# The second MLP product of five token groups by Strassen's identity, with its sums on VectorE and GpSimd

## The chip, the cores and the metric

The kernel runs on one core of a Trainium2 chip. The metric is the device time of one execution in microseconds (us). The profile's own time is its span, from the first to the last instruction of one profiled execution. The engines are TensorE (PE, whose weight loads are listed as PEld), VectorE (DVE), ScalarE (ACT), GpSimd (POOL) and SyncE (SP), which only issues transfers here.

## The reference

A block-wise linear attention with decay feeds a two-layer MLP. Batch 4, 8 heads, 768 positions, head size 64; the MLP sees 3072 tokens of width 512 and has 2048 hidden units.

```
for b in range(nb):                              # per head, blocks of positions
    intra = (q_b @ k_b.T * Dmask) @ v_b          # Dmask[i, j] = lam ** (i - j) for i >= j
    out_b = intra + (q_b * lam ** (pos + 1)) @ state
    state = lam ** block * state + (k_b * lam ** (block - 1 - pos)).T @ v_b
x = out as 3072 x 512                            # heads side by side
g = gelu(x @ w_in)                               # w_in 512 x 2048, exact gelu
result = g @ w_out                               # w_out 2048 x 512, f32
```

## The kernel before

The tokens are cut into 24 chunks of 128, six to a batch element, and four chunks make a group (`M = 4`, `NG = 6` groups of 512 tokens). A group's attention output, transposed, is `xT[g]`, four tiles of 128 features by 512 tokens in bf16.

`mlp_blocks(g)` gives the MLP of a group as a list of blocks, each with a cost by which the work is ordered. The first product has 16 blocks, `mm1(kf)`: four matmuls of 128x512 into a PSUM bank (L288) and a Gelu on ScalarE into `g_t`, bf16, 16 tiles of 128 hidden units by 512 tokens (L290). The second product takes `g_t` as the weights of PE and `w_out_t` as the moving operand: for each chunk of 128 tokens, 16 matmuls of 128x512 (L300), a copy to SBUF on ScalarE (L305) and a store of 256 KB on SP's queue (L306). The last chunk of the last group is done in two halves of 256 columns (L315, L319, L320).

Attention for group g + 1 is woven into the MLP of group g. The order of all instructions is that in which the code writes them; nothing is rescheduled, so each engine runs its own part of that one order as its queue, and waits on semaphores. The main loop runs through the blocks, adds up their costs in `done`, and emits a step of attention when `done` passes its mark. Marks are fractions of a group's total cost. For chunk n, the i-th of its group, with `at = 0.06 + 0.245 * i`:

- kind 0, at `at - 0.32` (earlier in the group before for small i): `dma_transposes` has SP transpose k (L189), GpSimd scale q to `q_hat` (L190), and SP transpose that (L191); GpSimd decays k to `k_dec` (L167); `prefetch` issues the three loads of a chunk three further on from GpSimd (L65).
- kind 2, at `at`: `scores` (PE L198; the masks on VectorE, L202) and `next_state` (PE L238; VectorE L245 and L246).
- kind 3, one chunk later (0.965 for the last): `outputs` (PE L253, L263), emptied by a cast on VectorE into `xT[g + 1]` (L273).

PSUM has eight banks: two each for the tags `sc`, `mh` (first product) and `mo` (second product), one for `o` (attention output) and one for `t` (state). Group 0 has another order, written out by hand, and its own weaving of the attention of group 1; it isn't touched.

Of the kernel before, what the change touches and what calls it, by code (L numbers as in the profile page):

```python
# [8 lines left out]
F32 = mybir.dt.float32  # L9
BF16 = mybir.dt.bfloat16  # L10
ALU = mybir.AluOpType
# [4 lines left out]
def kernel(  # L16
# [10 lines left out]
    nc = tc.nc  # L27

    B, H, S, D = q.shape
    d_model, d_ff = moe_w_in.shape  # L30
# [18 lines left out]
    work_pool = ctx.enter_context(tc.tile_pool(name="work", bufs=3))  # L49
    x_pool = ctx.enter_context(tc.tile_pool(name="x", bufs=2))  # L50
    g_pool = ctx.enter_context(tc.tile_pool(name="g", bufs=2))
    out_pool = ctx.enter_context(tc.tile_pool(name="outp", bufs=3))
    ps = ctx.enter_context(tc.tile_pool(name="ps", bufs=1, space=bass.MemoryType.PSUM))


# [92 lines left out]
    def bank(shape, dtype, tag, name):  # L148
        return ps.tile(shape, dtype, tag=tag, name=name, bufs=2 if tag in ("sc", "mh", "mo") else 1)
# [123 lines left out]
            nc.vector.tensor_copy(c.x_o, c.o_ps)  # L273


    def mlp_blocks(g):
        T = M * C
        x_t = xT[g]
# [16 lines left out]
        def mm2(io, part):  # L295
            def run():
                if part == 0:
                    om[io] = bank([128, d_model], F32, "mo", "o2_ps")
                for kf in range(part * 4, part * 4 + 4):
                    nc.tensor.matmul(om[io], g_t[:, kf, io * C:(io + 1) * C], w_out_t[:, kf, :],  # L300
                                     start=(kf == 0), stop=(kf == NK2 - 1))
                if part == NK2 // 4 - 1:
                    o_sb = out_pool.tile([128, d_model], F32, tag="o_s", name="o_sb")
                    r = (g * M + io) * C
                    nc.scalar.copy(o_sb, om[io])  # L305
                    nc.sync.dma_start(out[r:r + C, :], o_sb)  # L306
            return run

        def mm2_half(io, half):

            def run():
                w = slice(half * (d_model // 2), (half + 1) * (d_model // 2))
                o2 = bank([128, d_model // 2], F32, "mo", "o2_ps")
                for kf in range(NK2):
                    nc.tensor.matmul(o2, g_t[:, kf, io * C:(io + 1) * C], w_out_t[:, kf, w],  # L315
                                     start=(kf == 0), stop=(kf == NK2 - 1))
                o_sb = out_pool.tile([128, d_model // 2], F32, tag="o_h", name="o_sb")
                r = (g * M + io) * C
                nc.scalar.copy(o_sb, o2)  # L319
                nc.sync.dma_start(out[r:r + C, w], o_sb)  # L320
            return run

        parts = NK2 // 4
        blocks = [(mm1(kf), 4 * T) for kf in range(NK2)]
        if g == 0:

            blocks += [(mm2(io, part), 4 * 512) for pair in range(0, M, 2) for part in range(parts)
                       for io in (pair, pair + 1)]
        else:
            last = g == NG - 1  # L330
            blocks += [(mm2(io, part), 4 * 512) for io in range(M - last) for part in range(parts)]
            if last:
                blocks += [(mm2_half(M - 1, half), 16 * 256) for half in range(2)]
        return blocks


# [84 lines left out]


    total = NK2 * 4 * M * C + M * NK2 * 512
    x1 = lambda n: outputs(live[n], xT[1], n - M)
    group0 = {
        1: [lambda: next_state(live[3])],
# [12 lines left out]
    for n in range(2 * M, NCH):  # L439
        g, i = n // M - 1, n % M  # L440
        at = 0.06 + 0.245 * i
        fs = [at - (0.18 if n == 2 * M else 0.32), None, at, at + 0.245 if i < M - 1 else 0.965]
        todo += [(round((g + f) * total), -kind, n) for kind, f in enumerate(fs) if f is not None]
    todo.sort()

    def step(minus_kind, n):
# [58 lines left out]
```

## Time and profile before

| | |
|---|---|
| three runs | 217.22, 218.49, 219.40 us; median 218.49 |
| span of the profiled execution | 217.5 us; no time of that execution other than its span is given |
| PE busy | 204.9 us, 94% |
| PE weight loads busy | 102.9 us, 47% |
| GpSimd busy | 105.8 us, 49% |
| ScalarE busy | 91.1 us, 42% |
| VectorE busy | 74.8 us, 34% |
| mean granted TensorE clock | 0.997 |
| groups 1, 2, 3, 4, 5 start at | 54.0, 89.2, 121.6, 153.8, 186.2 us |

Busy times are unions of the instructions' intervals on an engine. A matmul's own duration in the trace (0.377 us for 128x512) is longer than its share of the time, since matmuls overlap in the array; the price of a matmul in a stream is the distance of two starts. "Idle before" a group of instructions is followed by what ended the idle time. GpSimd's work is front-loaded: it runs ahead as far as its buffers let it, and has nothing left to do after 152 us.

### The profile page before, as it was taken

The page shows a single profiled execution, that of the slowest core. Times are in us where ns is not written, and L with a number is a line of the kernel's source. Part 1 is how long each engine was busy: PE and PEld are TensorE (multiplying, and loading weights), DVE is VectorE, ACT ScalarE, POOL GpSimd, SP SyncE. Part 2 cuts the span into 40 slices and gives each one's busy share as a digit, 9 for nine tenths or more (in the row PEclk, how much of TensorE's full clock was granted, in tenths as well). Part 3 has the DMA queues.
Part 4 walks back from the last instruction along what each step waited for, and adds up shares of the span by engine and source line. Part 5 has one row for each costly group of instructions (what it writes and reads, how often), then busy time and mean ns, then how long its engine had stood idle before and what let it go on. Part 6 is the DMA issues. An engine that isn't in the chain of part 4 may idle for free.

```text
span 217.5 us, 3545 instructions
## 1 busy us (share of the span) xinstructions
PE 204.9 (94%) x1422; PEld 102.9 (47%) x1446; DVE 74.8 (34%) x120; ACT 91.1 (42%) x169; POOL 105.8 (49%) x120
## 2 busy tenths in 40 slices
PE   7679999999987999999999999999999999999993
PEld 2355444555443544444545444544445545444452
DVE  5884000478516243316225323315415323100000
ACT  6975772434563321365221375221465221566121
POOL 8998333998999999276950809113000000000000
PEclk9999999999999999999999999999999999999998
DMA  5999999999999999999999497515251012100112
GB/s 37 149 169 203 198 194 183 156 208 148 177 150 126 164 128 138 215 110 104 109 114 160 77 180 62 37 48 146 74 98 24 3 57 88 50 0 3 48 49 96
DMA packets 100272, 24.35 MB, mean 112 GB/s; under 512 B 92960, under 2 KB 97312, under 8 KB 100256
## 3 DMA queue, kind: packets, MB, share of 16 engines
q0 software_dynamic: 79104, 13.64, 84.4%
q1 hardware_dynamic: 21152, 10.50, 22.7%
q8 instruction: 11, 0.18, 0.3%
q14 instruction: 5, 0.04, 0.1%
HBM read 27.27 MB, written 6.29 MB: 154 GB/s over the span
## 4 chain that ended last, share of the span: by engine, by line
PE 73%; DMA 14%; POOL 9%; issue 2%; ACT 0%; POOLq 0%
PE o_ps L300 33%; PE h_ps L288 28%; DMA q_t<-in_q_dram 8%; DMA qT<-q_hat 3%; DMA w_in_t<-in_moe_w_in_dram 3%; PE o_ps L263 3%; PE sc_ps L198 3%; POOL k_t L65 3%; POOL q_t L65 2%; POOL v_t L65 2%; PE kv_ps L238 2%; PE o_ps L315 2%; PE o_ps L253 2%; POOL k_dec L167 1%; POOL q_hat L190 1%
## 5 line engine op out<-in xcount | busy, mean ns | idle before, releaser
L288 PE MATMUL h_ps<-x_t,w_in_t 128*128 128x512 bf16 (+2 forms) x378 | 84.8, 377 | 1.0 <-DMA w_in_t<-in_moe_w_in_dram 0.5
L300 PE MATMUL o_ps<-w_out_t,g_t 128*128 128x512 bf16 x355 | 81.8, 379 | 0.8 <-issue 0.3
L290 ACT ACTIVATE g_t<-h_ps 128x512 bf16<-128x512 f32 x96 | 57.3, 597 | 35.3 <-PE h_ps L288 35.3
L288 PEld LDWEIGHTS <-w_in_t 128*128 128x128 bf16 x388 | 37.3, 98 | 43.8 <-DMA w_in_t<-in_moe_w_in_dram 0.6
L300 PEld LDWEIGHTS <-g_t 128*128 128x128 bf16 x368 | 34.7, 98 | 39.6
L305 ACT COPY o_sb<-o_ps 128x512 f32<-128x512 f32 x23 | 13.5, 586 | 68.3 <-PE o_ps L300 62.5
L202 DVE TENSOR_TENSOR sc_m<-sc_ps,dmask 128x512 bf16<-128x512 f32 x48 | 30.8, 683 | 16.1 <-PE sc_ps L198 15.8
L273 DVE CAST x_t<-o_ps 128x512 bf16<-128x512 f32 x16 | 11.1, 692 | 71.4 <-PE o_ps L263 71.4
L190 POOL TENSOR_TENSOR q_hat<-q_t,lam_p 128x512 bf16<-128x512 bf16 x16 | 16.9, 1056 | 20.0 <-DMA qT<-q_hat 19.0
L167 POOL TENSOR_TENSOR k_dec<-k_t,lam_m 128x512 bf16<-128x512 bf16 x16 | 17.7, 1106 | 14.0 <-PE kv_ps L238 8.1
L65 POOL DMA_DIRECT2D k_t<-in_k_dram x24 | 22.1, 920 | 4.0 <-DMA w_out_t<-in_moe_w_out_dram 2.1
L65 POOL DMA_DIRECT2D q_t<-in_q_dram x24 | 21.5, 897 | 4.2 <-DMA w_out_t<-in_moe_w_out_dram 3.4
L65 POOL DMA_DIRECT2D v_t<-in_v_dram x24 | 21.4, 894 | 3.4 <-DMA w_out_t<-in_moe_w_out_dram 1.7
L198 PE MATMUL sc_ps<-qT,kT 64*128 64x128 bf16 x192 | 9.5, 218 | 3.8 <-DMA qT<-q_hat 2.6
L246 DVE TENSOR_TENSOR state<-tmp,lam_blk 128x512 bf16<-128x512 f32 x13 | 12.1, 932 | 0.5
L183 DVE TENSOR_TENSOR qT<-t_ps,lam_q 128x512 bf16<-128x512 bf16 x8 | 5.5, 689 | 18.9 <-PE t_ps L174 18.7
L263 PE MATMUL o_ps<-sc_m,v_t 128*64 128x128 bf16 x192 | 10.1, 225 | 0.0
L198 PEld LDWEIGHTS <-kT 64*128 64x128 bf16 x192 | 5.7, 94 | 8.3 <-issue 4.7
L361 PE MATMUL idle_ps<-idle 128*128 128x512 bf16 x21 | 7.5, 473 | 1.2 <-DVE idle L94 1.2
L245 DVE TENSOR_TENSOR tmp<-kv_ps,state 128x512 f32<-128x512 f32 x12 | 8.2, 681 | 0.0
L180 ACT COPY kT<-t_ps 128x512 bf16<-128x512 bf16 x7 | 4.1, 579 | 9.4 <-PE t_ps L174 9.4
L263 PEld LDWEIGHTS <-v_t 128*64 128x64 bf16 x192 | 6.2, 109 | 3.3 <-issue 0.8
(57 smaller groups left out, 82.7 us busy)
## 6 DMA issues: line engine op xcount, KB each, us to landing
out_dram<-o_sb SPq DMA_DIRECT2D x23, 256.0 KB, 2.6
k_t<-in_k_dram POOLq DMA_DIRECT2D x24, 128.0 KB, 4.6
q_t<-in_q_dram POOLq DMA_DIRECT2D x24, 128.0 KB, 5.9
v_t<-in_v_dram POOLq DMA_DIRECT2D x24, 128.0 KB, 5.9
w_in_t<-in_moe_w_in_dram POOLq DMA_DIRECT2D x4, 512.0 KB, 7.9
w_out_t<-in_moe_w_out_dram POOLq DMA_DIRECT2D x4, 512.0 KB, 15.1
kT<-k_t SPq DMA_TRANSPOSE x16, 4.7
qT<-q_hat SPq DMA_TRANSPOSE x16, 4.0
```

The lines of the kernel that those rows point to most:

```text
L65: nc.gpsimd.dma_start(raw[n, name], chunk_of(name, n))
L167: eng.tensor_mul(c.k_dec, c.k, scale[:, :, None].to_broadcast((128, H, D)))
L190: nc.gpsimd.tensor_mul(q_hat, c.q, lam_p[:, :, None].to_broadcast((128, H, D)))
L198: nc.tensor.matmul(sc_ps[hi][:, hp, :], c.kT[p, hp, :], c.qT[p, hp, :], start=True, stop=True)
L202: nc.vector.tensor_mul(c.sc_m[:, :, hi, :], sc_ps[hi], dmask_r[:, :, hi, :])
L246: nc.vector.tensor_mul(new, tmp, lam_blk)
L263: nc.tensor.matmul(o_ps[hi * D:(hi + 1) * D, hp, :], c.v[:, 2 * hp + hi, :], c.sc_m[:, hp, hi, :], start=(c.sb == 0 and hp == 0), stop=Tru ...
L273: nc.vector.tensor_copy(c.x_o, c.o_ps)
L288: nc.tensor.matmul(h_ps[:, lo:hi], w_in_t[:, ki, kf * 128:(kf + 1) * 128], x_t[:, ki, lo:hi], start=(ki == 0 and lo == 0), stop=(ki == NK1 ...
L290: nc.scalar.activation(g_t[:, kf, :], h_ps, ACT.Gelu)
L300: nc.tensor.matmul(om[io], g_t[:, kf, io * C:(io + 1) * C], w_out_t[:, kf, :], start=(kf == 0), stop=(kf == NK2 - 1))
L305: nc.scalar.copy(o_sb, om[io])
```

## The change

The second product of groups 1 to 5 is a product of a 512 x 2048 and a 2048 x 512 matrix. The changed kernel cuts each into four blocks: tokens into halves of 256 (`lo`, `hi`), hidden units into halves of 1024 (8 tiles of 128, `KH = 8`), output columns into halves of 256 (`DH`). Instead of eight block products it forms seven, each 16 matmuls of 128x256: two token tiles `u`, eight k tiles. The factors are sums of blocks. Sums of `w_out` blocks (five, numbered 1, 3, 4, 6, 7) are formed once, on VectorE, in group 1, in two pieces each of 128 x 1024 elements. Sums of `g_t` blocks (five, numbered 1, 2, 5, 6, 7) are formed in every group on VectorE, in four pieces of 128 x 512 elements each, emitted behind the blocks of the first product whose Gelus they need; the last four pieces come behind the first half of product 3. All are bf16.

The products run in the order 3, 4, 5, 2, 1, 6, 7. In PSUM, 3 and 5 accumulate in one bank (`p`), 4 and 2 in one (`q`), 1 and 7 in one (`r`), and 6 has its own (`s`); `p` and `q` are banks of the tag `mo`, `r` and `s` of `mh`, which the next group's first product uses too. ScalarE copies a bank out when a product ends, and the same bank goes on with the next product while the copied value is used in f32 sums: four additions or subtractions of 128 x 512 elements a group, on VectorE in group 1 and on GpSimd in groups 2 to 5. The last two additions of a group read PSUM and are done on VectorE. A group stores two halves of 256 tokens (512 KB each) when product 6 and product 7 are done; in the last group the first half is stored in two parts. The marks of attention steps are fractions of the new, smaller total cost of a group (`place`).

```diff
-    out_pool = ctx.enter_context(tc.tile_pool(name="outp", bufs=3))
+    out_pool = ctx.enter_context(tc.tile_pool(name="outp", bufs=2))
+    sum_pool = ctx.enter_context(tc.tile_pool(name="sums", bufs=1))
...
+    W_SUMS = {1: (B11, B22, ALU.add), 3: (B12, B22, ALU.subtract), 4: (B21, B11, ALU.subtract),
+              6: (B11, B12, ALU.add), 7: (B21, B22, ALU.add)}
+    def w_out_sum(i, half):
...
+        nc.vector.tensor_tensor(wsum[i][:, half * n:(half + 1) * n, :], w_out_t[:, at(ka), da], w_out_t[:, at(kb), db],
+                                op=op)
...
+        G_SUMS = {6: (0, hi, 0, lo, ALU.subtract), 1: (0, lo, KH, hi, ALU.add), 2: (0, hi, KH, hi, ALU.add),
+                  5: (0, lo, KH, lo, ALU.add), 7: (KH, lo, KH, hi, ALU.subtract)}
+        def g_sum(i, k):
...
+            nc.vector.tensor_tensor(gsum[i][:, k:k + 2, :], g_t[:, ka + k:ka + k + 2, ta], g_t[:, kb + k:kb + k + 2, tb],
+                                    op=op)
+        def with_sums(kf, run):
+            def both():
+                run()
+                done = kf - 2
+                if done >= 1 and done % 2 == 1:
+                    if done < KH:
+                        g_sum(6, done - 1)
+                    else:
+                        for i in (5, 1, 2, 7):
+                            g_sum(i, done - 1 - KH)
+                if g == 1 and 2 <= kf < 12:
+                    w_out_sum(*w_sums_left.pop(0))
+            return both
...
+        def late_sums():
+            for i in (5, 1, 2, 7):
+                g_sum(i, KH - 2)
...
+        def product(i, u, key, begin):
+            o = banks[key][:, u, :]
+            for k in range(KH):
+                nc.tensor.matmul(o, left[i](k, slice(u * C, (u + 1) * C)), right[i](k),
+                                 start=(begin and u == 0 and k == 0), stop=(k == KH - 1), skip_group_check=True)
+        adder = nc.vector if g == 1 else nc.gpsimd
...
+        def m3(u):
...
+            product(3, u, "p", True)
+            if u == 0:
+                late_sums()
+            else:
+                nc.scalar.copy(tile_f("e"), banks["p"])
+        def m4(u):
...
+            product(4, u, "q", True)
+            if u == 1:
+                nc.scalar.copy(tile_f("f"), banks["q"])
+                adder.tensor_add(sb["e"], sb["e"], sb["f"])
+        def m5(u):
+            product(5, u, "p", False)
+            if u == 1:
+                sb["o0"] = out_pool.tile([128, 2, d_model], F32, tag="o0", name="o0_sb")
+                nc.scalar.copy(sb["o0"][:, :, d_hi], banks["p"])
+                adder.tensor_sub(sb["f"], sb["e"], sb["o0"][:, :, d_hi])
+                if last:
+                    store(0, sb["o0"], d_hi)
+        def m2(u):
+            product(2, u, "q", False)
+            if u == 1:
...
+                nc.scalar.copy(sb["o1"][:, :, d_lo], banks["q"])
+                adder.tensor_sub(sb["e"], sb["e"], sb["o1"][:, :, d_lo])
+        def m1(u):
...
+            product(1, u, "r", True)
+            if u == 1:
+                nc.scalar.copy(tile_f("m"), banks["r"])
+                adder.tensor_add(sb["m"], sb["m"], sb["e"])
+        def m6(u):
+            product(6, u, "s", True)
+            if u == 1:
+                nc.vector.tensor_add(sb["o1"][:, :, d_hi], banks["s"], sb["m"])
+                store(1, sb["o1"])
+        def m7(u):
+            product(7, u, "r", False)
+            if u == 1:
+                nc.vector.tensor_add(sb["o0"][:, :, d_lo], banks["r"], sb["f"])
+                store(0, sb["o0"], d_lo if last else slice(0, d_model))
+        blocks += [((lambda f=f, u=u: f(u)), KH * DH) for f in (m3, m4, m5, m2, m1, m6, m7) for u in range(2)]
...
-            last = g == NG - 1
-            blocks += [(mm2(io, part), 4 * 512) for io in range(M - last) for part in range(parts)]
-            if last:
-                blocks += [(mm2_half(M - 1, half), 16 * 256) for half in range(2)]
+        if g > 0:
+            return blocks_by_seven(g, g_t, blocks)
...
+    later = NK2 * 4 * M * C + 7 * 2 * KH * DH
+    def place(at):
+        g, f = int(at), at - int(at)
+        return round(f * total) if g == 0 else round(total + (g - 1 + f) * later)
...
-        todo += [(round((g + f) * total), -kind, n) for kind, f in enumerate(fs) if f is not None]
+        todo += [(place(g + f), -kind, n) for kind, f in enumerate(fs) if f is not None]
```

## The prediction

> **What bounds the kernel now.** I read the view by stages first, cut at the starts of the groups (columns: window, its length, then busy us and instruction count of each engine, granted TensorE clock, DMA share, GB/s).
>
> ```profile
> core 0: us, PE busy (x) PEld busy (x) DVE busy (x) ACT busy (x) POOL busy (x), PEclk, DMA share, GB/s
> 54.00:89.20 35.20, 32.43 (x219) 16.03 (x221) 14.01 (x19) 11.90 (x20) 32.61 (x35) 1.00 2.00 148
> 89.20:121.60 32.40, 32.19 (x218) 15.82 (x221) 12.60 (x19) 11.90 (x20) 19.52 (x21) 1.00 1.21 129
> 121.60:153.80 32.20, 31.99 (x214) 15.62 (x217) 10.82 (x17) 11.90 (x20) 12.83 (x14) 1.00 0.68 90
> 153.80:186.20 32.40, 32.08 (x218) 15.90 (x221) 11.50 (x18) 11.90 (x20) 0.00 (x0) 1.00 0.22 58
> 186.20:214.10 27.90, 27.72 (x143) 13.96 (x143) 0.00 (x0) 12.32 (x22) 0.00 (x0) 1.00 0.12 43
> ```
>
> From group 2 on PE is never idle for more than 0.4 us a group, so every microsecond of matmul removed there is a microsecond of span, as long as nobody else becomes late. Group 1 (54.0 to 89.2) is different: GpSimd is busy for 32.6 of its 35.2 us, and PE lost 2.8 us there (2.2 of it a wait for a transposing DMA). Next, the chain that ended last (start, length, what) and the page's row of the wide products, for the price of a matmul:
>
> ```profile
> 186.35 3.02 PE h_ps L288 x14
> 189.43 10.74 PE h_ps L288 x49
> 200.22 10.31 PE o_ps L300 x47
> 210.53 3.51 PE o_ps L315 x32
> 214.06 0.37 ACT o_sb L319
> ```
>
> 10.31/47 = 0.219 us is a little high because a record is missing; 48 matmuls of 512 columns in 10.31 us make 0.215. The 32 matmuls of 256 columns take 3.51/32 = 0.110 us each, each with its own weight load, so halving the width halves the price.
>
> **What the change takes from PE.** Per group the second product goes from 64 x 0.215 = 13.8 us to 112 x 0.110 = 12.3 us: 1.5 us in groups 1 to 4, 1.55 in group 5, together **-7.6 us**. I trust this term to 0.5 us.
>
> **What it adds to VectorE, and where that is late.** Per group 20 sums of 512 bf16 elements (five sums in four pieces) and two additions from PSUM; in group 1 also ten weight sums of 1024 elements and four f32 additions. No row shows an addition of two bf16 tiles. The bounds:
>
> ```profile
> L167 DVE TENSOR_TENSOR k_dec<-k_t,lam_k 128x512 bf16<-128x512 bf16 x1 | 0.7, 681 | 0.0
> L138 DVE TENSOR_TENSOR dmask<-cmask,lam_m 128x1024 f32<-128x1024 f32 x1 | 1.2, 1225 | 0.8 <-ACT lam_m L124 0.8
> L182 DVE COPY kT<-t_ps 128x512 bf16<-128x512 bf16 x1 | 0.4, 416 | 0.0
> ```
>
> L167 has an f32 factor and costs 0.68 for 512 elements; L182, whose operands are all bf16 as in the new sums, costs 0.42. I take L182's pace, and for 1024 elements 0.42 + (1.225 - 0.681)/2 = 0.69; the other end is 0.68 and 1.23. Consecutive instructions overlap by 0.08 (two L202 of 0.681 take 1.29 below), so pitches are 0.34, 0.61, and 0.60 for the 512-element f32 kind.
>
> Groups 2 to 5 have room. After the second chunk's scores in a group VectorE needs about 4 us for its cast, mask and state work, then 13 x 0.34 = 4.4 us to the last sum of product 5, which PE reaches 11.3 us after that same point (six first-product blocks 5.2, products 3 and 4 3.5, two steps of attention 1.2 to 1.3 each). Slack about 3 us: cost 0.
>
> **Group 1 has none.** VectorE and GpSimd in that group (start, length, engine, line):
>
> ```profile
> 58.66 1.54 DVE L246 TENSOR_TENSOR state<-tmp,lam_blk 128x512 bf16<-128x512 f32 x1
> 67.12 1.29 DVE L202 TENSOR_TENSOR sc_m<-sc_ps,dmask 128x512 bf16<-128x512 f32 x2 [1.87 <-PE sc_ps L198]
> 69.04 1.83 DVE L246 TENSOR_TENSOR state<-tmp,lam_blk 128x512 bf16<-128x512 f32 x1
> 77.47 0.97 DVE L246 TENSOR_TENSOR state<-tmp,lam_blk 128x512 bf16<-128x512 f32 x1
> ```
>
> ```profile
> 58.55 1.09 POOL L190 TENSOR_TENSOR q_hat<-q_t,lam_p 128x512 bf16<-128x512 bf16 x1
> 59.56 1.54 POOL L167 TENSOR_TENSOR k_dec<-k_t,lam_m 128x512 bf16<-128x512 bf16 x1
> 68.43 1.06 POOL L190 TENSOR_TENSOR q_hat<-q_t,lam_p 128x512 bf16<-128x512 bf16 x1
> 69.42 0.92 POOL L65 DMA_DIRECT2D k_t<-in_k_dram  x1
> 76.81 1.07 POOL L190 TENSOR_TENSOR q_hat<-q_t,lam_p 128x512 bf16<-128x512 bf16 x1
> 77.82 1.51 POOL L167 TENSOR_TENSOR k_dec<-k_t,lam_m 128x512 bf16<-128x512 bf16 x1
> ```
>
> L246 is the loop's only VectorE instruction with both inputs in SBUF; its undisturbed time is 0.69. At 58.66 it ends at 60.20, which is 0.69 after 59.51, 0.13 before the q_hat of 58.55 ended; at 77.47 it ends 0.69 after 77.75, again 0.13 before a q_hat ended; and the k_dec behind it took 1.54 and 1.51 in place of 1.05. L202 and L245, with one input in PSUM, stay at 0.68. So a VectorE instruction with two SBUF inputs and a GpSimd tensor instruction exclude each other, each about 0.95 us to the other. Every new sum is of that kind.
>
> VectorE's queue in the changed order of group 1, from 60.2 (chunk 8's state): 8 weight pieces and 4 of sum 6, 8 x 0.61 + 4 x 0.34 = 6.2; cast, two masks, tmp, state 3.2; 2 weight pieces and 13 sums, to the last of product 5, 1.2 + 4.4 = 5.6. Together 15.0, to 75.2. PE gets to product 5 at 72.45 (end of the first product in the trace) + 32 x 0.11 + 1.2 for chunk 9's outputs and chunk 10's scores = 77.2. Alone it would fit. But the trace has eight GpSimd tensor instructions in that stretch (59.56, 63.74, 64.75, 68.43, 72.12, 73.13, 76.81, 77.82); the one at 68.43 falls beside casts and masks, seven hold the sums up by 0.95: 6.6 us, to 81.8. PE waits **+4.6 us** (0 to 9 by the bounds: no exclusion, or every one of the DMA issues too). Behind the waiting sums stand the masks of chunk 10, needed 3.5 us later at product 1; they fit.
>
> PE idle for 4.6 us can also lose its clock. The profile shows full clock through the 2.2 us wait of this group, and half clock from 2.1 us after the last matmul (the last 3.4 us have a mean of 0.80); the first nine 512-column matmuls take 3.73 us, twice their later price. So the cost lies between 0 and 3.7/2 = 1.85; I take the middle, **+0.9**. The Trainium skill (TensorE: Matmul & The Clock Gate, Part 1) says a free-running window of 3.4 us must be idle; by that 4.6 us lose the clock one time in three, an estimate of 0.6 and a sum 0.3 lower. The 2.1 us above speak for the shorter time.
>
> **What it adds to GpSimd.** From group 2 on four f32 additions of 512 elements; nearest rows L190 and L167 at 1.05 (bounds 0.68, VectorE's, and 2.1, twice). In the changed order of groups 2 and 3, q_hat and k_dec of the next group's first chunk and three loads (0.9 each) stand between the second and the third addition. Counted from the end of product 5: ScalarE copy 0.59; subtraction to 1.65; q_hat, k_dec 3.75; loads 6.45; two additions 8.55; VectorE's o1 addition 9.25; behind it in VectorE's queue the cast of the last x block, 9.9. PE meanwhile: product 2 1.75, attention 1.2, product 1 1.75, product 6 1.75, half of 7, outputs 0.65, half of 7: 8.9. The next group's first matmul needs that cast: 1.0 us late in each of two groups, **+2.0** (0 to 8). Groups 4 and 5 have the additions unbroken: 0. Stores now go out late, ahead of transposes on SP's queue, but those have some 9 us before their scores.
>
> **The tail.** Last copy 0.37 becomes an addition of 0.69; the last store is 256 KB in place of 128 (landing 2.0 against 1.7 us by the rows of DMA issues), with 512 KB 1 us ahead of it: **+0.8** (0.3 to 2).
>
> ScalarE gets one copy more of 0.59 us per group while it is idle: 0. Sum: -7.6 + 4.6 + 0.9 + 2.0 + 0.8 = +0.7 on a span of 217.5, so 218.2; the shown median of 218.5 lies 1.0 above that span: **219.2**.
>
> **Rivals.**
> 1. *The sums slip in.* If GpSimd's instructions fall into VectorE's gaps, or hold it for less, the group 1 wait shrinks below 1 us and the clock stays: -7.6 + 0.5 + 2.0 + 0.8 = -4.3, **214.2**. For it: alone the queue fits with 2 us to spare. Against: four L246 collisions, none shorter than the rest of GpSimd's instruction.
> 2. *GpSimd's DMA issues exclude sums as well* (the other side, slower). At 69.04 L246 lasted until 70.87, though the q_hat ended at 69.49: 0.69 before its end is 70.18, near the end of the k_t issue (70.34). Another L246, at 53.45, ran undisturbed beside an issue. A dozen issues in the stretch, half of them holding 0.85: +5 us, **224.2**; from two more holds on the result is over 1% slower. The Trainium skill (SBUF — State Buffer, Who interferes with whom) infers that issuing needs only the write interface and does not exclude such a sum; the row at 69.04 does not fit that, the one at 53.45 does.
> 3. *The sums run at L167's pace.* Group 1: 8 x 1.15 + 4 x 0.6 + 3.2 + 2 x 1.15 + 13 x 0.6 = 24.9, to 85.1, with collisions of 7.6 to 92.7: a 15.5 us wait, 1.8 for the clock, 1.5 in each of groups 2 to 4. Sum +17, **235**.
> 4. *The change takes nothing from PE* (256 columns dearer than half). L315's rows exclude it but for a few tenths.
>
> **Chances.** Forecast 0.37 (within 1%, some 2.2 us, which is also the spread of the three runs shown, 217.2 to 219.4, and about what can be told from no change); rival 1 0.28 (faster); rival 2 0.25 and rival 3 0.08 (slower), 0.02 for others, slower. The range leaves out rival 3 and the extremes: it goes from 213.4, below rival 1, to 225.5, above rival 2. Faster 0.28, same 0.37, slower 0.35.
>
> **What would show it.** Second-product matmuls at 0.110 each, 112 of them a group; PE idle once in group 1, ahead of product 5, released by VectorE's sum 5, for 3 to 6 us; in groups 2 and 3 about 1 us ahead of the next first product, released by a cast; sums at 0.42 alone and up to 1.5 beside GpSimd. If product 5 does not wait, rival 1 has it; if L-rows of the sums average 0.7 or more with no GpSimd instruction beside them, rival 3; if they end with DMA issues, rival 2.

## The result and the profile after

The changed kernel takes **230.08 us** (median of four runs, 228.59 to 231.38), the kernel before 218.51 (four runs, 217.22 to 219.4). The ratio is 1.053 with a 95% interval from 1.047 to 1.058: 5% slower, and above the predicted range. The profiled execution took 231.38 us with a span of 229.4, 11.9 more than the span before; its mean granted clock is 0.969. All ratios here leave runs in a disturbed state out, which the medians don't, so that a ratio need not be that of the two medians; the two differ most in experiment 6 (median 213.56).

The view by stages of the changed kernel, cut at the starts of groups 1 to 5 and at PE's last matmul (columns as in the prediction: window, length, busy us and count of PE, PEld, DVE, ACT, POOL, granted clock, DMA share, GB/s):

```profile
54.86:99.14 44.28, 34.59 (x269) 21.73 (x268) 38.50 (x54) 13.06 (x22) 35.25 (x36) 0.88 1.54 117
99.14:131.98 32.84, 31.07 (x270) 20.53 (x268) 20.79 (x42) 12.48 (x21) 15.08 (x15) 1.00 0.68 83
131.98:166.66 34.68, 30.84 (x264) 20.30 (x264) 21.14 (x40) 12.48 (x21) 22.67 (x24) 1.00 1.15 107
166.66:199.07 32.41, 32.41 (x269) 21.15 (x269) 19.54 (x40) 12.48 (x21) 8.97 (x8) 0.95 0.28 62
199.07:225.40 26.33, 26.33 (x178) 17.12 (x175) 8.80 (x22) 12.48 (x21) 5.06 (x4) 1.00 0.13 47
```

Against the span before, cut the same way: group 1 begins 0.8 later and lasts 44.3 in place of 35.1 (+9.2); group 2 +0.4; group 3 +2.4; group 4 the same; group 5 -1.5; the rest behind the last matmul +0.6. Together +11.9. Only group 5, where no attention runs and GpSimd has nothing but the four additions, shows the whole gain of 1.5 us. In group 1 VectorE is busy for 38.5 of 44.3 us and GpSimd for 35.3, and PE, which was busy for 92% of that stage before, is busy for 78%.

PE's timeline of the changed kernel in group 1, at product 5 (start, length, line, out<-in, shapes, count, idle before and what ended it):

```profile
77.94 0.39 PE L345 MATMUL p_ps<-w_out_t,g_sum 128*128 128x256 bf16 x2 [0.90 <-DVE g_sum L311]
80.73 0.39 PE L345 MATMUL p_ps<-w_out_t,g_sum 128*128 128x256 bf16 x2 [2.40 <-DVE g_sum L311]
83.76 0.61 PE L345 MATMUL p_ps<-w_out_t,g_sum 128*128 128x256 bf16 x2 [2.64 <-DVE g_sum L311]
86.80 2.31 PE L345 MATMUL p_ps<-w_out_t,g_sum 128*128 128x256 bf16 x10 [2.43 <-DVE g_sum L311]
88.91 3.48 PE L345 MATMUL q_ps<-w_out_t,g_sum 128*128 128x256 bf16 x16
```

Product 5 waits four times, once for each piece of its sum, 8.4 us in all. Behind the waits the matmuls are slow: 16 matmuls of product 2 take 3.48 us, where the same 16 take 1.91 elsewhere (below, in the fourth experiment). The windows view, cut on a grid of 3.413 us (a half-clock stretch in the clock record begins at 81.87 and lasts 10.24 us, three times 3.413; another lasts 3.413 us from 167.20; the windows shown lie 0.05 us behind that grid):

```profile
78.51:81.92 3.41, 0.39 (x2) 0.11 (x2) 3.41 (x6) 0.00 (x0) 3.40 (x4) 0.99 1.56 99
81.92:85.33 3.41, 0.61 (x2) 0.13 (x2) 3.41 (x6) 0.00 (x0) 3.40 (x5) 0.50 0.94 60
85.33:88.75 3.42, 1.95 (x10) 1.39 (x11) 3.42 (x7) 0.00 (x0) 3.42 (x4) 0.50 1.15 76
129.70:133.11 3.41, 1.64 (x11) 0.84 (x10) 1.88 (x3) 0.01 (x1) 3.41 (x4) 1.00 0.70 120
163.83:167.24 3.41, 1.38 (x11) 0.86 (x9) 1.89 (x3) 0.00 (x0) 3.33 (x4) 0.99 0.97 85
167.24:170.65 3.41, 3.41 (x20) 1.39 (x18) 0.33 (x1) 1.19 (x2) 3.05 (x4) 0.50 1.10 313
```

The number behind the comma is PE's busy time. A window with 0.39 us of matmuls is followed by half clock; so is the one at 163.83, in which PE was busy for 1.38 us. The one at 129.70, with 1.64, is not. The windows of all fourteen traces, each cut on the grid of its own clock record, divide without an exception: of those at full clock, all 31 with 1.55 us of matmuls or less are followed by half clock (highest 1.54, in experiments 5 and 10) and none of the 821 with 1.59 us or more (lowest 1.59, in experiments 4 and 6). Of those at half clock, the five with 2.68 us or less stay there, and the 17 with 2.76 us or more are followed by full clock.

The windows at 129.70 and 163.83 hold waits at the starts of groups 3 and 4. PE's timeline of the changed kernel there and in between:

```profile
131.98 1.89 PE L427 MATMUL h_ps<-x_t,w_in_t 128*128 128x512 bf16 x8 [1.77 <-DVE x_t L274]
...
143.82 0.40 PE L199 MATMUL sc_ps<-qT,kT 64*128 64x128 bf16 x8 [1.82 <-DMA qT<-q_hat]
...
166.66 3.08 PE L427 MATMUL h_ps<-x_t,w_in_t 128*128 128x512 bf16 x8 [2.03 <-DVE x_t L274]
```

Both group starts wait for the cast of the last x block, and a chunk's scores in group 3 wait for a transpose of `q_hat`. GpSimd's timeline ahead of group 3, behind the second addition (L380, 122.08 to 123.34), and VectorE's:

```profile
123.30 1.04 POOL L191 TENSOR_TENSOR q_hat<-q_t,lam_p 128x512 bf16<-128x512 bf16 x1
124.30 1.04 POOL L168 TENSOR_TENSOR k_dec<-k_t,lam_m 128x512 bf16<-128x512 bf16 x1
125.29 0.92 POOL L66 DMA_DIRECT2D k_t<-in_k_dram  x1
126.20 0.90 POOL L66 DMA_DIRECT2D q_t<-in_q_dram  x1
127.09 0.88 POOL L66 DMA_DIRECT2D v_t<-in_v_dram  x1
127.98 1.28 POOL L389 TENSOR_TENSOR f_e<-f_e,o_sb 128x512 f32<-128x512 f32 x1
129.34 1.26 POOL L398 TENSOR_TENSOR f_m<-f_m,f_e 128x512 f32<-128x512 f32 x1
```

```profile
130.64 0.69 DVE L403 TENSOR_TENSOR o_sb<-s_ps,f_m 128x512 f32<-128x512 f32 x1 [3.27 <-POOL f_m L398]
131.25 0.68 DVE L274 CAST x_t<-o_ps 128x512 bf16<-128x512 f32 x1
```

This is the chain of the prediction: q_hat, k_dec and three loads between the second and the third addition, the last addition on VectorE behind the fourth, and the cast behind that. It ends at 131.93, 1.7 after PE ran out of work (130.21).

How VectorE came to be late in group 1 is in its own timeline and GpSimd's:

```profile
60.84 1.74 DVE L293 TENSOR_TENSOR w_sum<-w_out_t 128x1024 bf16<-128x1024 bf16 x1
62.51 1.26 DVE L311 TENSOR_TENSOR g_sum<-g_t 128x512 bf16<-128x512 bf16 x1
63.69 1.28 DVE L293 TENSOR_TENSOR w_sum<-w_out_t 128x1024 bf16<-128x1024 bf16 x2
...
79.41 8.34 DVE L311 TENSOR_TENSOR g_sum<-g_t 128x512 bf16<-128x512 bf16 x12
```

```profile
60.27 1.54 POOL L168 TENSOR_TENSOR k_dec<-k_t,lam_m 128x512 bf16<-128x512 bf16 x1
61.77 0.92 POOL L66 DMA_DIRECT2D k_t<-in_k_dram  x1
62.68 0.89 POOL L66 DMA_DIRECT2D q_t<-in_q_dram  x1
63.56 0.88 POOL L66 DMA_DIRECT2D v_t<-in_v_dram  x1
...
84.21 1.06 POOL L191 TENSOR_TENSOR q_hat<-q_t,lam_p 128x512 bf16<-128x512 bf16 x1
85.25 1.21 POOL L168 TENSOR_TENSOR k_dec<-k_t,lam_m 128x512 bf16<-128x512 bf16 x1
```

The weight sum at 60.84 takes 1.74 in place of 0.68: it waits out the k_dec of 60.27. The sum at 62.51 takes 1.26 in place of 0.41, and no GpSimd tensor instruction runs beside it: its 0.85 lie beside two load issues. The two sums at 63.69, beside another issue, are undisturbed (1.28 for two). Twelve sums from 79.41 take 8.34 us; alone they take 4.11.

### The profile page after: what moved, and what is told of

Read it like the earlier page. It is cut to its first block, busy times and chain, and to the rows that moved or that the text cites. A ratio compares the mean times of both kernels' runs of the same rounds, so it can differ in the third digit from the quotient of the medians.

```text
span 229.4 us, 4164 instructions
## 1 busy us (share of the span) xinstructions
PE 205.1 (89%) x1670; PEld 126.7 (55%) x1670; DVE 135.6 (59%) x244; ACT 93.8 (41%) x173; POOL 128.0 (56%) x136
## 4 chain that ended last, share of the span: by engine, by line
PE 61%; POOL 12%; DVE 12%; DMA 10%; issue 3%; ACT 0%; POOLq 0%; DVEq 0%; ACTq 0%
PE h_ps L427 27%; PE p_ps L345 7%; PE q_ps L345 7%; DMA qT<-q_hat 6%; PE o_ps L439 5%; DVE g_sum L311 5%; PE r_ps L345 5%; DVE w_sum L293 4%; DMA w_in_t<-in_moe_w_in_dram 4%; POOL k_t L66 3%; POOL v_t L66 2%; PE sc_ps L199 2%; PE s_ps L345 2%; POOL q_t L66 2%; PE o_ps L264 2%
## 5 line engine op out<-in xcount | busy, mean ns | idle before, releaser
L427 PE MATMUL h_ps<-x_t,w_in_t 128*128 128x512 bf16 (+2 forms) x388 | 86.8, 380 | 5.0 <-DVE x_t L274 3.8
L311 DVE TENSOR_TENSOR g_sum<-g_t 128x512 bf16<-128x512 bf16 x100 | 44.1, 498 | 15.6 <-ACT g_t L429 15.6
L345 PEld LDWEIGHTS <-g_sum 128*128 128x128 bf16 x400 | 39.5, 101 | 15.7 <-DVE g_sum L311 9.7
L373 POOL TENSOR_TENSOR f_e<-f_e,f_f 128x512 f32<-128x512 f32 x4 | 5.7, 1415 | 65.7 <-ACT f_f L372 65.7
L203 DVE TENSOR_TENSOR sc_m<-sc_ps,dmask 128x512 bf16<-128x512 f32 x48 | 30.8, 682 | 15.7 <-PE sc_ps L199 15.4
L345 PE MATMUL r_ps<-w_sum,g_sum 128*128 128x256 bf16 x160 | 19.8, 273 | 0.0
L345 PE MATMUL p_ps<-w_out_t,g_sum 128*128 128x256 bf16 x80 | 11.3, 294 | 8.4 <-DVE g_sum L311 8.4
L345 PEld LDWEIGHTS <-g_t 128*128 128x128 bf16 x160 | 15.5, 98 | 2.8
L184 DVE TENSOR_TENSOR qT<-t_ps,lam_q 128x512 bf16<-128x512 bf16 x8 | 5.5, 687 | 18.9 <-PE t_ps L175 18.7
L439 PE MATMUL o_ps<-w_out_t,g_t 128*128 128x512 bf16 x64 | 15.5, 380 | 0.0
L403 DVE TENSOR_TENSOR o_sb<-s_ps,f_m 128x512 f32<-128x512 f32 x5 | 3.5, 692 | 18.0 <-POOL f_m L398 17.6
L345 PE MATMUL q_ps<-w_out_t,g_sum 128*128 128x256 bf16 x80 | 11.1, 300 | 0.0
```

What stands on the lines that cost most here:

```text
L203: nc.vector.tensor_mul(c.sc_m[:, :, hi, :], sc_ps[hi], dmask_r[:, :, hi, :])
L311: nc.vector.tensor_tensor(gsum[i][:, k:k + 2, :], g_t[:, ka + k:ka + k + 2, ta], g_t[:, kb + k:kb + k + 2, tb], op=op)
L345: nc.tensor.matmul(o, left[i](k, slice(u * C, (u + 1) * C)), right[i](k), start=(begin and u == 0 and k == 0), stop=(k == KH - 1), skip_gr ...
L427: nc.tensor.matmul(h_ps[:, lo:hi], w_in_t[:, ki, kf * 128:(kf + 1) * 128], x_t[:, ki, lo:hi], start=(ki == 0 and lo == 0), stop=(ki == NK1 ...
```

## The experiments

The experiments start from the changed kernel. Each was compared with runs of the kernel before on the same chip (medians 217.55 to 218.16); ratios are against those.

**1. The four f32 additions on VectorE in all groups.** It takes the additions out of GpSimd's queue.

```diff
-        adder = nc.vector if g == 1 else nc.gpsimd
+        adder = nc.vector
```

> The four f32 additions of groups 2 to 5 go from GpSimd to VectorE, as in group 1; nothing is left out. Queue theory (the third and fourth addition stand behind q_hat, k_dec and three loads on GpSimd): the waits for the cast ahead of groups 3 and 4 (1.8 and 2.0 us), the 1.8 us wait for a transposed q_hat in group 3 and the half clock at the start of group 4 (1.7 us) go, group 1 stays as it is: 230.1 - 7.3 = about 223 us. Rival (the last cast is late because of the PSUM additions ahead of it on VectorE, or because of the banks): VectorE has 4 x 0.6 us more to do per group, the waits stay: 230 to 232 us.

Measured: 226.38 us, ratio 1.039 (1.034 to 1.044), 3.7 us below the changed kernel. The wait ahead of group 4, the half clock behind it and the wait for q_hat in group 3 are gone. The wait ahead of group 3 stays, 1.96 us, and now costs a window of half clock. Its cause has changed. VectorE's and GpSimd's timelines of this kernel:

```profile
121.27 1.53 DVE L373 TENSOR_TENSOR f_e<-f_e,f_f 128x512 f32<-128x512 f32 x1
122.91 2.49 DVE L380 TENSOR_TENSOR f_f<-f_e,o_sb 128x512 f32<-128x512 f32 x1
```

```profile
116.57 2.56 POOL L191 TENSOR_TENSOR q_hat<-q_t,lam_p 128x512 bf16<-128x512 bf16 x1
...
122.78 1.07 POOL L191 TENSOR_TENSOR q_hat<-q_t,lam_p 128x512 bf16<-128x512 bf16 x1
123.79 1.05 POOL L168 TENSOR_TENSOR k_dec<-k_t,lam_m 128x512 bf16<-128x512 bf16 x1
```

The subtraction at 122.91 takes 2.49 in place of 0.69: it waits through a q_hat and the k_dec behind it. In turn the q_hat of 116.57, issued into a row of VectorE sums, takes 2.56 in place of 1.04. Moving the additions to VectorE takes the chain away and puts collisions in its place, so that about half of the expected gain is given back.

**2. The weight sums in group 0.** It relieves VectorE in group 1 by some 6.1 us of its own work.

```diff
-                if g == 1 and 2 <= kf < 12:
-                    w_out_sum(*w_sums_left.pop(0))
...
+                if i == NK2:
+                    for half in range(2):
+                        for j in W_SUMS:
+                            w_out_sum(j, half)
```

> The ten weight sums are formed on VectorE in group 0, before the block at which its second product starts, instead of among the first product's blocks of group 1; nothing is left out. Theory (product 5 of group 1 waits because VectorE's queue is too long once GpSimd's instructions push in): 6.1 us of VectorE's own time and three or four collisions leave group 1, the 8.4 us of waits ahead of product 5 go down to under 1.5 us, the 10 us at half clock go too (2.9 us of loss), up to 1 us is lost in group 0: about 220 us. Rival (each of the 16 last sums is late by itself, by collisions with GpSimd, and the weight sums only come earlier): at least 5 us of waits stay, and the clock falls: 225 us or more.

Measured: 226.18 us, ratio 1.034 (1.027 to 1.041), nearer to the rival. Product 5 still waits, 1.35 + 1.80 us, and a window of half clock follows. In group 0 chunk scores wait 1.28 us for a scaled qT that VectorE makes (L184), now behind the sums. VectorE's timeline of this kernel shows why product 5 is still late:

```profile
69.28 14.31 DVE L311 TENSOR_TENSOR g_sum<-g_t 128x512 bf16<-128x512 bf16 x16
```

16 sums that take 5.4 us alone take 14.3. Six GpSimd tensor instructions run in that time, and the six sums that meet them lose 5.5 of the 8.9 us. Four further sums of 1.26 us (at 69.61, 73.55, 74.74 and 78.62) lie beside load issues alone; they make up the other 3.4.

**3. Both of these edits.**

> Both edits together, nothing left out. Theory: the two lossy places are independent, so that what is left is the gain on PE and the tail: 218.5 - 7.6 + 0.6 to 0.8, plus up to 1 us in group 0: 211.5 to 213 us, faster than the kernel before by 2.5 to 3%. Rival (one late queue takes the place of the other: VectorE with 4 more additions per group): 216 us or more.

Measured: 220.84 us, ratio 1.010 (1.003 to 1.018). The two gains more than add up (3.7 and 3.9 to 9.2 us), but the whole stays 8 to 9 us above what the theory wanted. In the profile, of an execution of 222.70 us, product 5 waits 2.57 + 0.73 us, and group 3 starts after a wait of 1.96 behind additions of 1.53 and 2.49 us, as in the first experiment. What is left looks less like the amount of work on either engine than like the two standing in each other's way; the next experiment and the eighth test that.

**4. No GpSimd tensor work beside the sums of group 1.** Chunks 9 to 15 use q and k as loaded; the loads stay.

```diff
-        nc.gpsimd.tensor_mul(q_hat, c.q, lam_p[:, :, None].to_broadcast((128, H, D)))
+        if 9 <= c.n < 16:
+            q_hat = c.q
+        else:
+            q_hat = work_pool.tile([128, H, D], BF16, tag="qh", name="q_hat")
+            nc.gpsimd.tensor_mul(q_hat, c.q, lam_p[:, :, None].to_broadcast((128, H, D)))
...
+            if 9 <= n < 16:
+                live[n].k_dec = live[n].k
+            else:
+                decay_k(live[n], nc.gpsimd)
```

> The changed kernel, but for chunks 9 to 15 q and k are used as loaded: GpSimd's q_hat and k_dec (two tensor instructions a chunk) are left out, its DMA issues stay. Exclusion theory: VectorE's own 15 us from chunk 8's state to the last sum of product 5 fit, all sums at 0.42 and 0.69; product 5 waits under 1.5 us, the clock stays full: about 219 to 220 us. Rival (VectorE's own pace, without GpSimd): the waits stay above 5 us: 226 us or more. Rival (DMA issues exclude the sums too): sums of 1.2 us beside issues, and 2 to 5 us of waits: 222 to 226 us.

Measured: 218.88 us, ratio 1.003 (0.998 to 1.008), as the theory has it: 11 us below the changed kernel for 13 GpSimd instructions left out (seven q_hat, and six k_dec, since chunk 11 has none), 12 of which run in the stage of group 1 in the changed kernel. The groups of lines of this kernel between 56 and 84 us (busy us, mean ns, idle before), beside the changed kernel's own in group 1 (from 54.86 to 92.2):

```profile
L314 DVE TENSOR_TENSOR g_sum<-g_t 128x512 bf16<-128x512 bf16 x20 | 7.2, 419 | 0.0
L296 DVE TENSOR_TENSOR w_sum<-w_out_t 128x1024 bf16<-128x1024 bf16 x10 | 6.6, 685 | 0.0
```

```profile
L311 DVE TENSOR_TENSOR g_sum<-g_t 128x512 bf16<-128x512 bf16 x20 | 13.9, 750 | 0.0
L293 DVE TENSOR_TENSOR w_sum<-w_out_t 128x1024 bf16<-128x1024 bf16 x10 | 10.2, 1038 | 0.0
```

Without tensor work on GpSimd all 30 sums run at their own pace, at a mean of 0.419 and 0.685 us, though 12 load issues lie beside them (60.22 to 76.16). With it they take 10.1 us more. PE's timeline of this kernel:

```profile
75.98 1.91 PE L348 MATMUL p_ps<-w_out_t,g_sum 128*128 128x256 bf16 x16
77.73 1.91 PE L348 MATMUL q_ps<-w_out_t,g_sum 128*128 128x256 bf16 x16
```

Product 5 runs without a wait, and the distance of the two starts, 1.75 us for 16 matmuls, is the price of 0.109 each. So none of these load issues held a sum; where issues did, in the changed kernel and in experiment 2, there was tensor work around them. The waits ahead of groups 3 and 4 and for a q_hat in group 3 (1.77, 2.03 and 2.43 us), which the edit does not touch, are still there.

**5. No loads after chunk 11.** Chunks 12 to 23 use the q, k, v of chunks 4 to 11; 36 load issues fall away.

```diff
-        c.q, c.k, c.v = (raw.pop((n, name)) for name in "qkv")
+        src = n if n < 12 else 4 + (n - 4) % 8
+        c.q, c.k, c.v = (raw[src, name] for name in "qkv")
...
-        while next_load[0] <= min(upto, NCH - 1):
+        while next_load[0] <= min(upto, 11):
```

> The changed kernel, but chunks 12 to 23 use the q, k, v of chunks 4 to 11: 36 loads and so nearly all of GpSimd's DMA issues from 62 us on are left out, its tensor instructions (q_hat, k_dec) stay. Theory (beside GpSimd tensor work the DMA issues hold sums up too, some 3 us of the lateness in group 1): product 5 waits 4 to 6 us in place of 8.4, 224 to 226 us. Rival (tensor instructions alone hold sums up; issues cost nothing): the waits stay at 7 to 9 us, 228 us or more, but for what less DMA traffic gives elsewhere (1.8 us in group 3).

Measured: 220.61 us, ratio 1.011 (0.999 to 1.023), faster than both expected, so it doesn't settle what it was meant to in group 1. What it did settle is in groups 2 to 4: no wait over 0.6 us is left at their starts or for a q_hat, so the three loads are a needed part of the chain ahead of the casts. In group 1 GpSimd now has its tensor instructions back to back and earlier. VectorE's and GpSimd's timelines of this kernel:

```profile
60.60 3.52 DVE L294 TENSOR_TENSOR w_sum<-w_out_t 128x1024 bf16<-128x1024 bf16 x1
```

```profile
60.03 1.54 POOL L169 TENSOR_TENSOR k_dec<-k_t,lam_m 128x512 bf16<-128x512 bf16 x1
61.54 1.03 POOL L192 TENSOR_TENSOR q_hat<-q_t,lam_p 128x512 bf16<-128x512 bf16 x1
62.54 1.03 POOL L169 TENSOR_TENSOR k_dec<-k_t,lam_m 128x512 bf16<-128x512 bf16 x1
```

One weight sum waits 2.8 us, through three GpSimd instructions in a row: a VectorE instruction that waits isn't always let in when the next of GpSimd's follows at once. (In the changed kernel the sums of 64.89, 79.41 and 84.30 were, between a q_hat and the k_dec behind it, which then took 1.21 us in place of 1.04.) A wait of 2.34 us for a cast came with that, product 5 waited 2.6.

**6. The products alone.** All sums and the four f32 additions are left out, and blocks stand in for them.

> The seven products, copies, PSUM additions and stores stay, every sum of blocks of g and w_out and the four f32 additions a group are left out (blocks stand in their place). If the products give what the 256-column price says and all else is the sums: 218 - 7.6 + 0.6 (tail) = 211 us. Rival (the products themselves, their banks or copies cost more than priced): 214 us or more.

Measured: ratio 0.969 (0.957 to 0.981), from 210.47 and 212.58 us, near 211. Against 217.55 that is 5 to 7 us, and the predicted -7.6 with a tail of 0.6 makes -7.0: PE's gain is there to be had. The interval is wide, and no more is read from it.

**7. PE kept busy through the wait.** In group 1 three times eight matmuls of zeros, 512 columns into a bank of the tag `mh`, stand ahead of product 5's later pieces. They shorten no wait.

```diff
+            if g == 1 and i == 5 and u == 0:
+                warm_ps = bank([128, 512], F32, "mh", "warm_ps")
             for k in range(KH):
+                if g == 1 and i == 5 and u == 0 and k in (2, 4, 6):
+                    for _ in range(8):
+                        nc.tensor.matmul(warm_ps, idle[:, :128], idle, start=True, stop=True)
```

> In group 1 three times eight 512-column matmuls of zeros stand inside the first half of product 5, ahead of its third, fifth and seventh matmul, where PE waits for sums; nothing is left out. Theory: the waits stay (8 us of PE time, now partly filled), the 10 us at half clock go, and with them 2.9 us: 227 us. Rival (the half clock costs nothing of its own since VectorE is behind anyway, or the zeros come on top of the waits): 230 us or more.

Measured: 227.86 us, ratio 1.045 (1.036 to 1.055), 2.2 us below the changed kernel; the two intervals overlap, so the time alone would not decide. PE's timeline of this kernel does:

```profile
83.51 1.89 PE L349 MATMUL warm_ps<-idle 128*128 128x512 bf16 x8
86.32 1.26 PE L350 MATMUL p_ps<-w_out_t,g_sum 128*128 128x256 bf16 x10 [0.92 <-DVE g_sum L311]
87.42 1.91 PE L350 MATMUL q_ps<-w_out_t,g_sum 128*128 128x256 bf16 x16
```

The last piece of the sum comes as late as before, but product 2 takes 1.91 in place of 3.48 and the ten matmuls ahead of it 1.26 in place of 2.31; the granted clock is 1.00 from 76 to 94 us. The clock is a cost of its own: 1.57 + 1.05 us by these rows. The 2.2 us of the medians are less sure, since a wait that the zeros don't touch, that for a q_hat in group 3, also differs between the two profiled executions (1.82 and 0.66 us).

**8. Everything on VectorE.** The edits of the first two experiments, and q_hat and k_dec of the steps of the main loop on VectorE too. From group 2 on GpSimd has only loads.

```diff
-        nc.gpsimd.tensor_mul(q_hat, c.q, lam_p[:, :, None].to_broadcast((128, H, D)))
+        nc.vector.tensor_mul(q_hat, c.q, lam_p[:, :, None].to_broadcast((128, H, D)))
...
-            decay_k(live[n], nc.gpsimd)
+            decay_k(live[n], nc.vector)
```

> Weight sums in group 0, the f32 additions, q_hat and k_dec of chunks 8 to 23 (without 5 to 7, whose k_dec stays) on VectorE in all groups: GpSimd keeps only its DMA issues in groups 1 to 5; nothing is left out. Theory (exclusion is the cause, VectorE alone has room: about 25 of 31 us a group): no wait for a sum over 1 us, clock full, 211.5 to 213.5 us, faster than before by 2 to 3%. Rival (VectorE becomes the bound with 4.8 us more a group): waits ahead of product 5 in every group, 217 us or more.

Measured: 215.72 us, ratio 0.989 (0.981 to 0.997): 1.1% faster than the kernel before, though 2.2 us above the upper end of the theory, with more work on VectorE than in any kernel so far. The group of the sums in this kernel, and the stage of group 3:

```profile
L311 DVE TENSOR_TENSOR g_sum<-g_t 128x512 bf16<-128x512 bf16 x100 | 36.0, 418 | 13.6 <-ACT g_t L427 13.5
```

```profile
123.16:153.84 30.68, 30.58 (x264) 20.26 (x264) 25.63 (x50) 12.48 (x21) 0.66 (x1) 1.00 0.48 74
```

All hundred sums run at 0.418, the changed kernel's at a mean of 0.498; groups 3 and 4 last 30.7 and 30.8 us, 1.5 less than before, with VectorE busy for 25.6 us of one. What is still lost in this execution lies elsewhere. Group 1 begins at 57.84 in place of 54.05: PE waits 2.22 us for a load of w_in at 21.06, where it waited 0.47 in the kernel before, and a window of half clock follows, which costs 1.7. That wait stands ahead of every instruction that the edits touch; the other traces have anything from under 0.25 to 2.87 us there, so it is a difference between executions and no price of the weight sums. Transposes of q_hat are waited for 1.48 and 1.96 us in groups 1 and 2, while the loads still run.

**9. As 8, with the weight sums in group 1 where the change has them.**

> As the run with all on VectorE, but the ten weight sums are back in group 1, as in the changed kernel; nothing is left out. Theory: without GpSimd tensor work group 1 takes the weight sums nearly without a wait (15.0 us of VectorE's own time and three or four pieces of q_hat and k_dec, 18 us, against 17 that PE leaves), product 5 waits 0.5 to 1.5 us, and group 0 gets back the 1 to 2 us that the sums cost it: 214 to 215.5 us. Rival (one VectorE queue can't hold all in group 1): waits of 3 us or more, 217 us.

Measured: 217.26 us, ratio 0.995 (0.991 to 0.999). That is the rival's time, but not its mechanism: the profile, of the fastest of the twelve executions (215.32 us), shows no wait at product 5. Group 1 begins at 55.23, but waits of 1.97 and 0.74 us for transposes of q_hat come in it, the first with a window of half clock behind it. With experiment 8 its interval overlaps: where the weight sums stand doesn't decide any more.

**10 and 11. The transposes' marks earlier, in 9 and in 8.**

```diff
-        fs = [at - (0.18 if n == 2 * M else 0.32), None, at, at + 0.245 if i < M - 1 else 0.965]
+        fs = [at - (0.18 if n == 2 * M else 0.32 if n < 3 * M else 0.42), None, at, at + 0.245 if i < M - 1 else 0.965]
```

> The run with late weight sums, and the mark of the transposes of chunks 12 to 23 moved from 0.32 to 0.42 of a group ahead of their scores, so that they stand ahead of the group's stores on SP's queue; nothing is left out. Theory: the 2 us wait for a transposed q_hat in group 2 goes: 1.5 to 2 us less than the run with late weight sums, about 212.5 to 213.5 us. Rival (the transposes wait for loads or are slowed by DMA traffic, not by the queue): no difference.

> The run with all on VectorE (weight sums in group 0), with the same earlier marks; nothing is left out. Theory: 215.7 - 1.5 to 2 = about 214 us; with the weight sums in group 0 it stays some 1 us slower than with them in group 1. Rival: group 0 costs nothing and group 1 does, then this is the fastest of the three, about 213 us.

Measured: 217.61 us, ratio 0.996 (0.993 to 1.000), and 215.97, ratio 0.990 (0.985 to 0.994): no difference from 9 and 8. The edit does what it should where it applies: the wait of 1.96 us ahead of chunk 13's scores in experiment 8 is gone in 11. In its place waits for casts appear (0.52 and 0.65 us in 10, 0.88 and 0.65 in 11). The waits for transposes that stay, 2.16 and 1.87 us (in 10) and 2.11 (in 11), lie in group 1 ahead of the scores of chunks 8 and 11, whose marks the edit does not move. What makes those late stayed open; an earlier mark for them was not tried.

**12. Seven products only from group 2 on.** Group 1 keeps the plain second product, the weight sums run beside it on VectorE, and from chunk 12 on q_hat and k_dec are on VectorE, as are all additions.

```diff
-        if g > 0:
+        if g > 1:
             return blocks_by_seven(g, g_t, blocks)
+        if g == 1:
+            return blocks + [(mm2(io, part), 4 * 512) for io in range(M) for part in range(parts)]
...
+            if g == 1 and 17 <= i < 27:
+                w_out_sum(*w_sums_left.pop(0))
```

> Seven products only in groups 2 to 5; group 1 has the plain product, as before, and the ten weight sums stand on VectorE among its second product's blocks; the f32 additions, and q_hat and k_dec of chunks 12 to 23, are on VectorE (chunks 8 to 11 stay on GpSimd); nothing is left out. Theory (the losses left in the all-on-VectorE runs are in groups 0 and 1, where the sums and q_hat meet GpSimd's loads and a late transpose): group 1 is as long as before, 35.1 us, groups 2 to 4 30.7 to 31 each, group 5 26.2, tail +0.6: 218 - 4 x 1.5 + 0.6 = 212 to 213.5 us. Rival (DMA traffic in groups 0 and 1 costs what it costs, and the product of group 1 gave its 1.5 us): 217 us or more.

Measured: 215.01 us, ratio 0.987 (0.983 to 0.991), the fastest of the kernels that leave nothing out, by a little (the intervals of experiments 8 and 11 overlap with it): 1.3% faster than the kernel before and some 6% faster than the change. It stays 1.5 us above the upper end of the theory.

## Why the prediction was wrong, step by step

- **PE's gain, -7.6: right.** Starts of 16 matmuls are 1.75 us apart (0.109 each against 0.110 predicted), group 5 is 1.5 us shorter, and so are groups 3 and 4 where nothing waits (experiment 8).
- **The price of a bf16 sum: right.** 0.42 and 0.69 were taken; alone they take 0.418 and 0.683 to 0.685 (experiments 4 and 8). Rival 3 is out, and so is rival 4.
- **Exclusion between a VectorE instruction with two SBUF inputs and a GpSimd tensor instruction: right in kind.** Experiment 4 takes the one away and the other is undisturbed.
- **The wait at product 5, +4.6: mis-sized; it was 8.4.** (Experiment 1 has the same instructions in group 1, and there the waits add up to 6.8, so 8.4 is the size of one execution.) PE came to product 5 at 77.04 (predicted 77.2). VectorE should have delivered the last piece at 81.8 and did so at 86.8. 0.6 of the 5.0 us is a later start (60.8). 10.8 us were lost in holds ahead of that piece, against 6.6: 10.1 on the 30 sums (their busy times less those of experiment 4, by the means) and 0.7 on two state updates; one hold lengthened a sum by 0.85 (1.26 against 0.41). Seven tensor instructions up to the k_dec of 80.36 held sums, as many as predicted. Two more, those of 84.21 and 85.25, came into play only because VectorE was already late: in the trace before they start at 81.98 and 82.98, just behind the 81.8 at which the step had VectorE done, so that any further lateness had to meet them. And three sums (62.51, 76.62, 81.78) were held 0.85 each while only load issues ran: 2.5 us of rival 2. The Trainium skill (SBUF — State Buffer, Who interferes with whom) infers that an issue does not hold such a sum; experiment 4 agrees (30 sums, 12 issues beside them, none held), these three sums don't. Each of them lies beside the first two issues behind a k_dec, but in experiment 2 the sum of 69.61 was held beside issues with no k_dec ahead of them. By what rule is open.
- **The clock, +0.9: mis-sized and incomplete.** In group 1 the half clock lasted 10.24 us, not one stretch of 3.4: by the rows of 1.91 and 3.48, of 1.26 and 2.31, and of 0.39 and 0.61 it cost 2.8 us (2.2 by the medians of experiment 7), over the bound of 1.85, which was one window's. The step asked how long PE is idle in one piece; what divides the windows of the traces is how much matmul work a window of the 3.413 us grid holds (at most 1.55 us: the clock falls; at most 2.68 us at half clock: it stays down). The 2.1 us that the step read off the end of the kernel before fit this too: the window that ended there, at 216.13, held 1.31 us of matmuls. The wait was in four pieces with little matmul work between them, so that three windows in a row stayed sparse (0.39, 0.61 and 1.9 us); experiment 7 fills the four windows from 74.26 to 87.92 with 2.5 to 2.7 us of matmuls each and keeps the clock. And the clock fell a second time, ahead of group 4, for which the sum had no term at all: 8 matmuls in 3.08 against 1.89, with two small steps 1.6 us. The Trainium skill (TensorE: Matmul & The Clock Gate, Part 1) has the clock fall after an idle window of about 3.4 us; its length and free-running grid are what the trace shows (3.413 and 10.24), but the window before the second fall held 1.38 us of matmuls, so it need not be idle.
- **GpSimd's chain ahead of groups 3 and 4, +2.0: the mechanism was right, the size half of what it was: 1.77 + 2.03.** PE's side was right within 0.2 us. The additions took 1.26 to 1.28 in place of 1.05, three of them in the chain: 0.65 of the 0.8 missing in the first. The 1.05 was that of rows with a bf16 operand. The same lateness has a second end that the step didn't name: q_hat and k_dec stand behind the additions in GpSimd's queue, and the scores that need them waited 1.82 us in group 3. "A transpose has some 9 us before its scores" was said of stores on SP's queue, not of what feeds the transpose. With the additions gone from GpSimd (experiment 1) the wait ahead of group 4 and this one are gone; with the loads gone (experiment 5) all three are.
- **Sums in groups 2 to 5 at no cost: right for PE** (no wait for a sum there), and the tail, +0.8, was +0.6.

By stages: -7.6 for PE, +8.7 for sums and one mask in group 1, +4.4 for the clock, +3.8 for the two casts, +1.8 for q_hat, +0.6 for the tail, +0.8 for the start of group 1, and -1.5 since waits for transposes in group 1 are shorter now (2.56 us before, 1.03 after). That is +11.0 of 11.9. Of the 0.9 left, 0.5 is that product 5, broken into four pieces, keeps PE busy for 2.43 us at full clock and not for 1.91; 0.4 isn't placed. The +0.8 is no effect of the change: PE waits 1.23 us for a load of w_in at 20.29, ahead of all that was changed, where it waited 0.47 before.

Of the prediction as a whole, the terms were right in sign, and in place but for the second fall of the clock and the wait for q_hat in group 3, which it didn't have. The three large costs came out at about twice their size (8.7 and 3.8 against 4.6 and 2.0) or more (4.4 against 0.9). Their errors were not independent: a longer hold makes VectorE later, which lets in more GpSimd instructions and leaves PE's windows so sparse that they lose the clock. The range was built from single rivals, each with the other terms at their middle, and so left out that they grow together.

Experiment 8 shows for groups 3 and 4 that the sums themselves can be had for nothing (30.7 and 30.8 us, the whole gain of 1.5 us each), and experiments 4 and 8 together that the change loses by the division of work between VectorE and GpSimd more than by its added work. What keeps the best version 1.5 us or more above what PE's gain alone would give was not settled; apart from that for w_in, the longest waits left in the profiles of experiments 8 to 12 are for transposes of q_hat, in groups 1 and 2, while the loads run.

## What to carry to other kernels

When a change gives VectorE work with two SBUF inputs, look at what GpSimd does in the same stretch before counting either engine's room: here 13 GpSimd instructions of 1 us, all but one of them in one stage, cost 11 us, and moving all such work onto the busier VectorE was faster than sharing it. Price a contended wait by letting it run: as long as the waiting engine is late, further collisions come in, and a stretch with little matmul work costs PE its clock as well, even where no single wait in it is long. When an engine gets new work ahead of old, ask for each old instruction behind it who waits for that.

## What the runs showed of the hardware that was not expected

- A waiting VectorE instruction can be passed over by several GpSimd instructions in a row (2.8 us through three, experiment 5), though it isn't always (three sums of the changed kernel got in between two), and a q_hat on GpSimd by several VectorE sums (2.56 us for 1.04, experiment 1).
- Load issues on GpSimd held no sum where GpSimd did nothing else (12 issues beside 30 sums, experiment 4), but three sums of the changed kernel and four of experiment 2 were held 0.85 us beside issues that stand among tensor work.
- PE's clock fell after a wait of only 2.03 us, and came back a whole number of windows later: 3.413 and 10.24 us. In all fourteen traces the matmul time within a window of 3.413 us on the clock's grid tells what follows: 1.55 us or less at full clock is followed by half clock, 1.59 or more is not; 2.68 us or less at half clock keeps it, 2.76 or more ends it. So the same wait of 2 us can cost the clock or not, by where it falls on the grid: one of 1.97 us in experiment 9 did, one of 2.16 us in experiment 10 did not.
- An f32 addition of 512 elements takes 1.26 us on GpSimd and 0.69 on VectorE.
